# Two attention tiles per visit or one, and blocks of 256 or 512 tokens: a replanned order in a fused scan and two-layer MLP kernel

## The chip, the cores and the metric

The kernel runs on one core of a Trainium2 chip. The metric is the device time of one execution in microseconds; lower is better. The engines are named as in the profile: PE is the matrix engine (PEld its weight loads), DVE, ACT and POOL are the vector, scalar and GpSimd engines, SP is the engine whose queue issues most transfers.

## What is computed

Three stages follow each other on 3072 tokens (batch 4 by sequence 768) of 256 features. The scan works on 8 heads of 32 features with a state of 16 and chunks of 32 tokens; its output feeds the first layer, and that of the first the second, both 256 to 2048 to 256.

```python
# scan, per chunk of 32 tokens
la = log_a[:, :, sl]; cum = np.cumsum(la, axis=-1)
L = np.exp(cum[:, :, :, None] - cum[:, :, None, :]) * causal
M = np.einsum('bhin,bhjn->bhij', Cc, Bc) * L
y[:, :, sl] = M @ xc + np.einsum('bhin,bhnd->bhid', Cc, state) * np.exp(cum)
state = exp(sum(la)) * state + sum_j(B_j x_j * exp(cum[-1] - cum_j))
# layer 1
h = x @ w_in;  g = h * (1.0 / (1.0 + np.exp(-h)));  y = g @ w_out
# layer 2
h = x @ w_in2
P = a[0] + a[1]*h + a[2]*h**2 + a[3]*h**3
Q = 1.0 + abs(b[0])*abs(h) + abs(b[1])*h**2
out = (P / (Q + 1e-6)) @ w_out2
```

The weights come as 64-bit floats. Products are made from a high and a low part of each operand, three matmuls for one.

## The kernel before

**Tiles.** The tokens are cut into 24 tiles of 128, six per batch element. A tile's scan needs POOL and DVE passes (bw; ce, which multiplies by the decay factors; cx; cw), the small matmuls cb and u on PE, and on DVE the masked products M (L671, with the mask Gm of L589), the masked inputs um (L692) and the states S (L707, L709). A *visit* on PE then makes the tile's output from M and S (`att<-M,tok` and `att<-tok,S` in the profile). ACT writes its high part, y1h (L814), DVE its low part, y1l (L817). From visit 5 on, a visit also does cb and u of the tiles of the next visit. VISITS lists which tiles a visit takes: single tiles up to number 7, then pairs.

**Weights.** Each layer has 16 slices of 128 hidden units, 512 KB each. ACT (L490), DVE (L496, L498) and ACT and DVE or POOL (L514, L518) turn a slice into its high and low part; layer 2's slices are written to DRAM (w2s) in that form and loaded again later.

**Layer 1.** BLOCKS groups the tiles: two blocks of 256 tokens and five of 512. For each block and each slice there is an in-projection of six matmuls (`h<-y1h,w`, `h<-y1l,w`), silu on ACT (L900), the split into gh and gl (L856, L862), and an out-projection of six (`acc<-gh,w`, `acc<-gl,w`). Below, such six matmuls are a *group*. Layer 2 has the same shape over six blocks of 512, with ACT, POOL and DVE passes for P, Q and their quotient (DVE lines L968 to L986, twice or more per slice).

**Decay factors.** Per tile, 134 factors per partition, Ee, are needed. For tiles 0 to 2 they are made directly; for the others two products are written to DRAM (dre), and 21 loads of 67 KB, into a ring of four buffers, fetch them (L580).

**The order.** Everything is put into a Plan: an operation with its possible engines, an assumed length, a key, the buffers that it makes and uses. The planner lists the operations by assumed times, and this list is what each engine executes. K holds the numbers from which the keys come. A ring gives out its buffers in turn, and a turn also waits for the first user of the turn before. All transfers at the start are issued by SP, in the order of their keys; the helper `mm` (L290) issues every matmul.

Of the kernel before, what the change touches and what calls it, by code (L numbers as in the profile page):

```python
# [11 lines left out]
AF = mybir.ActivationFunctionType  # L12
# [13 lines left out]
BLOCKS = [2, 2, 4, 4, 4, 4, 4]  # L26
E_DIRECT = 3
NB2 = 512
# [3 lines left out]
    t0=-2912.149,  # L32
    step0=7.448,
    lag1=-799.401,
    fo1=18.905,
    fo2=5644.62,
    fol=22.648,
    tab=-142.05,
    lead=1708.414,
    kt=430.738,  # L40
    kq=-1089.363,
    kl=958.617,
    kg=5975.296,
# [15 lines left out]
    w1=-2845.877,
    w1step=-459.066,  # L60
    w1load=-38.315,
    tokload=151.165,
    ahead=-52.038,
    eps=0.021,
    step2=852.892,
    dT=[244.778, -4327.46, -1277.81, 3.30798e+06, -1852.19, 6.575, 6049.41, 42.655, 11.659, 525.288, -927.012, -29.398, 1118.15, -7033.22, -147.429, -1383.28, 639.647, -92.11, -499.629, -298.276, 63.339, -194.545, 195.77, -178.741],
    dD=[-3949.64, 1922.71, 516.55, -1.95112e+06, -295.737, 604.675, -1987.05, -321.034, -222.002, 1481.65, -774.684, 9639.86, -277.217, -203.799, 192.388, 31257.8, -1529.13, 49.425, -312.61, 173.525, 91.326, 298.355, 2.378, 3.702],
    dW=[1541.58, -222.487, -81.764, 7155.04, -53.883, 106.916, -69.667, -107.809, -443.948, 604.658, -226.317, -95.072, 42.853, 104.916, 101.819, 28.904],
# [17 lines left out]
IN_PSUM = 2  # L86
ALONE = 5
PAIRED = 8
# [30 lines left out]
class Plan:  # L119


    LAT = {"PE": 0.2, "ACT": 0.08, "DVE": 0.08, "POOL": 0.08, "SP": 2.0}
# [11 lines left out]
    def run(self):  # L134
# [3 lines left out]
        for op in self.ops:  # L138
            deps = set(op.deps)
            for b in op.new:  # L140
                i = b.ring.turns.index(b)
                if i:
                    deps.update(b.ring.turns[i - 1].users[:1])
                if i >= b.ring.n:
                    deps.update(b.ring.turns[i - b.ring.n].users)
            deps.discard(op)
            op.waits = deps
            left[op] = len(deps)
            for d in deps:
                waiting.setdefault(d, []).append(op)  # L150
# [73 lines left out]
def ssd_moe_moe_kernel(ctx: ExitStack, tc: tile.TileContext, tok, la_in, consts, w1, w2, ab, outT):  # L224
# [67 lines left out]
    def dma(key, nbytes, fn, deps=(), new=(), use=()):  # L292
        return add({"SP": (max(0.06, nbytes / 345e3), fn)}, key, deps, new, use)
# [26 lines left out]
    ring("Ee", 4, P + R6, pad=26)  # L320
# [34 lines left out]
    ld_la = dma(0.0, 98e3, lambda: (load_table(SET_LN_EXP), nc.sync.dma_start(la, la_in)))  # L355
# [7 lines left out]
    ld_c2 = dma(0.9, 66e3, lambda: nc.sync.dma_start(con[:, C_MASK:C_CUM], consts[:, C_MASK:C_CUM]))  # L363
    ld_ab = dma(0.95, 3e3, lambda: nc.sync.dma_start(abt, ab))
# [49 lines left out]
    o_ee, o_dre, dre = {}, [], fixed("dre", [P, 2, P + R6], space="DR")  # L414
    Ees = {}

    def factors(la_cols, key, after, use=()):
        Ee, pe = new("Ee"), new("h")

        def f_em():  # L420
            pe.t = pe.make()
            mm(pe.t[:, 0 : P + R6], la_cols(), difs, True, True)

        def f_ee():
            Ee.t = Ee.make()
            ACT.activation(Ee.t, pe.t[:, 0 : P + R6], AF.Exp)

        a = add({"PE": (c_mm32(P + R6), f_em)}, key, [o_ln, ld_c1] + after, new=[pe], use=list(use), cols=4 * (P + R6))
        return Ee, add({"ACT": (c_act(P + R6, True), f_ee)}, key, [a], new=[Ee], use=[pe])

    for n in range(E_DIRECT):
# [123 lines left out]
    def attention(n, T, d, k_load):  # L555
# [4 lines left out]
        def f_load():  # L560
            t.t = t.make()
            nc.sync.dma_start(t.t[:, 0:TOK], tok[n])
# [7 lines left out]

        if n < E_DIRECT:
            Ee = Ees[n]
        else:
            Ee = new("Ee")
            i = 0 if n < P // H else 1
            r = (n - i * (NTB - P // H)) * H

            def f_er():
                Ee.t = Ee.make()
                nc.sync.dma_start(Ee.t, dre[r : r + H, i, :].unsqueeze(1).broadcast_to([H, N, P + R6]))  # L580

            o_ee[n] = dma(k_load, 68e3, f_er, [o_dre[i]], new=[Ee])
        e0 = lambda: Ee.t[:, P : P + R6]
# [3 lines left out]
        def f_gm(eng):  # L587
# [10 lines left out]
            T, [o_eG[n], ld_c2], new=[Gm],  # L598
# [9 lines left out]
        def f_ce(eng):  # L608
            eng.tensor_tensor(cw(), cw(), Ee.t[:, 0:P], op=ALU.mult)  # L609
# [52 lines left out]
    def masked(n, cb, o_cb):  # L662
        t, T, d, ld, o_bw, o_cx, o_cw, o_gm, Gm, x, bw, cw, bt, cx, e0, Ee = at[n]
# [22 lines left out]
    def state(n, ub, o_u):  # L686
        t, T, d, ld, o_bw, o_cx, o_cw, o_gm, Gm, x, bw, cw, bt, cx, e0, Ee = at[n]
# [9 lines left out]
        a = add({"DVE": (c_dve(NCH * SW), f_um)}, T + 4.4 * d, [o_u, ld_c2], new=[um], use=[ub], rd=[2, 3])  # L697
        before = states.get(n - 1) if c else None
        here = [before]
        for i in range(NCH if c < TPB - 1 else 1):  # L700
# [11 lines left out]
            b = add({"DVE": (c_dve(SW, ap=1), f_s, True)}, T + 4.5 * d, deps, new=[sn], use=[um] + ([Ee, pv[0]] if pv else []))  # L712
# [58 lines left out]
    def visit(ns):  # L771
# [3 lines left out]
        if n < ALONE:  # L775
# [5 lines left out]
            o_y = add({"PE": (y_len, f_y)}, T + 5 * d, y_deps, new=ybs, use=y_use, wr=range(4), cols=y_cols, big=False)  # L781
# [3 lines left out]
        else:  # L785
# [3 lines left out]
            def f_visit():  # L789
# [7 lines left out]
                {"PE": (y_len + (0.25 + 0.35 * len(after) if after else 0.1), f_visit)}, T + 5 * d,  # L797
# [391 lines left out]
```

## Time and profile before

| | us |
|---|---|
| median of 3 runs (610.09 to 611.59) | 610.37 |
| profiled execution, its own time | 609.46 |
| span of its profile | 607.7 |
| mean granted clock of TensorE | 0.98 |

The profiled execution's time is 1.8 us longer than the span, which runs from its first instruction to its last. Busy times overlap across engines; a PE that is busy may still be working at a lower granted clock, so a stage is read by its busy time, its clock and its waits together.

### The profile page before, as it was taken

What the parts mean: (1) busy time and instruction counts of PE and PEld (TensorE: products, weight loads), DVE (VectorE), ACT (ScalarE), POOL (GpSimd) and SP (SyncE); (2) the same over time, 40 slices, a digit from 0 to 9 for tenths busy, and PEclk for the clock granted to TensorE, in tenths of its full rate; (3) what the DMA queues carried; (4) which work ended last, traced back from release to release, by engine and by line L of the source; (5) the groups of instructions that cost most, each with busy time, mean ns of one, the idle gap of its engine ahead of it and who ended that gap; (6) DMA issues with size and microseconds to landing.
All of it is one profiled execution on the core that took longest, in us unless ns stands there. A gap on an engine that the chain in (4) does not pass through costs nothing.

```text
span 607.7 us, 12571 instructions
## 1 busy us (share of the span) xinstructions
PE 582.2 (96%) x4778; PEld 479.4 (79%) x4781; DVE 435.2 (72%) x800; ACT 437.3 (72%) x858; POOL 280.8 (46%) x313
## 2 busy tenths in 40 slices
PE   7698888988999999999999999999999999999997
PEld 4377788867888888888888888888888888888886
DVE  5988875867852232232222799999999999999995
ACT  4677665755554444444444898998999999999994
POOL 2444323232320010010010589989877787877873
PEclk7889999989999999999999999999999999999999
DMA  6855556374610000000015710000000000000000
GB/s 210 277 182 173 199 212 235 134 265 158 218 73 0 1 0 1 0 2 0 1 69 159 281 46 2 0 36 1 25 12 1 36 1 0 36 0 2 35 1 35
DMA packets 18325, 47.38 MB, mean 78 GB/s; under 512 B 2009, under 2 KB 5465, under 8 KB 18265
## 3 DMA queue, kind: packets, MB, share of 16 engines
q1 hardware_dynamic: 18264, 46.58, 22.4%
q8 instruction: 37, 0.61, 0.4%
q14 instruction: 24, 0.19, 0.1%
HBM read 34.90 MB, written 11.67 MB: 77 GB/s over the span
## 4 chain that ended last, share of the span: by engine, by line
PE 88%; DVE 2%; issue 2%; ACT 2%; DMA 1%; SPq 0%; DVEq 0%; ACTq 0%
PE acc L290 43%; PE h L290 35%; PE b L290 7%; PE att L290 3%; DMA wraw<-in_w_dram 1%; DVE wv L498 1%; ACT wv L490 1%; DVE w L518 0%; ACT y1h L814 0%; ACT w L514 0%; ACT h L900 0%; DVE gl L862 0%; DVE y1l L817 0%; DVE M L671 0%; DVE tok L609 0%
## 5 line engine op out<-in xcount | busy, mean ns | idle before, releaser
L290 PE MATMUL h<-y1h,w 128*128 128x512 f32 (+1 forms) x700 | 229.3, 374 | 6.8 <-DVE gl L862 2.8
L290 PE MATMUL acc<-gh,w 128*128 128x512 f32 (+1 forms) x832 | 211.8, 377 | 0.1
L290 PEld LDWEIGHTS acc<-gh,w 128*128 128x128 f32 x832 | 151.1, 191 | 28.6 <-ACT gh L856 0.3
L290 PEld LDWEIGHTS h<-y1h,w 128*128 128x128 f32 x700 | 130.5, 190 | 32.9 <-DVE gl L862 4.1
L862 POOL TENSOR_TENSOR gl<-g,gh 128x512 fp32r<-128x512 f32 x95 | 122.9, 1294 | 25.1 <-ACT gh L856 22.9
L862 DVE TENSOR_TENSOR gl<-T,gh 128x512 fp32r<-128x512 f32 x71 | 50.0, 704 | 114.8 <-ACT gh L856 112.1
L290 PE MATMUL h<-y1l,w 128*128 128x512 f32 (+1 forms) x350 | 130.1, 372 | 0.8 <-DVE y1l L817 0.5
L290 PE MATMUL acc<-gl,w 128*128 128x512 f32 (+1 forms) x416 | 122.4, 375 | 0.0
L900 ACT ACTIVATE T<-h 128x512 f32<-128x512 f32 x80 | 47.8, 597 | 73.1 <-PE h L290 66.8
L290 PEld LDWEIGHTS acc<-gl,w 128*128 128x128 f32 x416 | 76.8, 190 | 14.0
L965 POOL TENSOR_SCALAR tok<-T,abt 128x512 f32<-128x512 f32 x96 | 74.1, 772 | 22.0 <-ACT T L957 20.9
L858 POOL TENSOR_SCALAR gh<-T 128x512 fp32r<-128x512 f32 x10 | 6.8, 676 | 166.8 <-PE acc L290 163.9
L290 PEld LDWEIGHTS h<-y1l,w 128*128 128x128 f32 x350 | 66.6, 190 | 11.8 <-DVE y1l L817 0.7
L968 DVE SCALAR_TENSOR_TENSOR b<-T,absb,b 128x512 f32<-128x512 f32 x96 | 72.3, 754 | 1.9 <-ACT b L961 0.5
L986 DVE SCALAR_TENSOR_TENSOR g<-tok,abt,b 128x512 f32<-128x512 f32 x96 | 71.1, 742 | 0.3
L977 ACT ACTIVATE b<-b,lnb 128x512 f32<-128x512 f32 x96 | 65.8, 685 | 2.3 <-DVE b L968 1.6
L856 ACT ACTIVATE gh<-T 128x512 fp32r<-128x512 f32 x70 | 44.2, 631 | 25.2 <-PE acc L290 25.1
L980 ACT ACTIVATE b<-b 128x512 f32<-128x512 f32 x96 | 59.7, 622 | 0.5
L856 ACT ACTIVATE gh<-g 128x512 fp32r<-128x512 f32 x71 | 47.5, 670 | 1.6 <-DVE g L986 1.5
L974 DVE SCALAR_TENSOR_TENSOR tok<-T,abt,h 128x512 f32<-128x512 f32 x63 | 46.7, 742 | 0.0
L290 PE MATMUL b<-y1h,w 128*128 128x512 f32 x132 | 46.1, 390 | 0.0
L971 DVE TENSOR_TENSOR h<-tok,h 128x512 f32<-128x512 f32 x63 | 43.4, 689 | 0.0
(72 smaller groups left out, 660.3 us busy)
## 6 DMA issues: line engine op xcount, KB each, us to landing
wraw<-in_w_dram SPq DMA_DIRECT2D x32, 512.0 KB
w2s<-wraw SPq DMA_DIRECT2D x16, 512.0 KB
w<-w2s SPq DMA_DIRECT2D x16, 512.0 KB
tok<-in_tok_dram SPq DMA_DIRECT2D x24, 320.0 KB
out_dram<-wraw SPq DMA_DIRECT2D x12, 256.0 KB
Ee<-dre SPq DMA_DIRECT2D x21, 67.0 KB
cum<-in_consts_dram SPq DMA_DIRECT2D x1, 192.0 KB
dre<-Ee SPq DMA_DIRECT2D x2, 67.0 KB
```

What stands on the lines that cost most here:

```text
L290: PE.matmul(out, lhsT, rhs, start=start, stop=stop)
L856: ACT.activation(gh.t[:, 0:W], g.t[:, 0:W], AF.Copy)
L858: eng.tensor_scalar(gh.t[:, 0:W], g.t[:, 0:W], 1.0, 0.0, op0=ALU.mult, op1=ALU.add)
L862: eng.tensor_tensor(gl.t[:, 0:W], g.t[:, 0:W], gh.t[:, 0:W], op=ALU.subtract)
L900: ACT.activation(T.t[:, 0:W], h.t[:, 0:W], AF.Silu)
L965: POOL.tensor_scalar(t1.t[:, 0:W], s.t[:, 0:W], abt[:, 3:4], abt[:, 1:2], op0=ALU.mult, op1=ALU.add)
L968: DVE.scalar_tensor_tensor(c.t[:, 0:W], s.t[:, 0:W], absb[:, 1:2], c.t[:, 0:W], op0=ALU.mult, op1=ALU.add)
L971: DVE.tensor_tensor(h.t[:, 0:W], t1.t[:, 0:W], h.t[:, 0:W], op=ALU.mult)
L974: DVE.scalar_tensor_tensor(t1.t[:, 0:W], s.t[:, 0:W], abt[:, 2:3], h.t[:, 0:W], op0=ALU.mult, op1=ALU.add)
L977: ACT.activation(c.t[:, 0:W], c.t[:, 0:W], AF.Ln, bias=lnb)
L980: ACT.activation(c.t[:, 0:W], c.t[:, 0:W], AF.Exp, scale=-1.0)
L986: DVE.scalar_tensor_tensor(g.t[:, 0:W], t1.t[:, 0:W], abt[:, 0:1], c.t[:, 0:W], op0=ALU.add, op1=ALU.mult)
```

## The change

It sets six blocks of 512 tokens in layer 1 (SH, the number of 256-token blocks, becomes 0, and IN_PSUM with it) and one tile per visit throughout. All decay factors lie in one fixed tile, Ea; tiles 0 to 2 are made there directly, and four loads bring the rest, for tiles 3 to 5, 6 to 9, 10 to 15 and 16 to 23. The layout of dre is by head and tile. The transfer of cum and of tile 0 is issued on ACT's queue, ahead of its table load; con comes in one transfer. The rule of the rings waits for the start, not the end, of the first user of the turn before. Assumed lengths of transfers and visits are a little higher, and the numbers of K are others (two of some hundred are shown). The lines of the changed kernel are 4 to 9 higher, so `mm` is L294 there.

```diff
-BLOCKS = [2, 2, 4, 4, 4, 4, 4]
+BLOCKS = [4, 4, 4, 4, 4, 4]
+SH = 2 if BLOCKS[:2] == [2, 2] else 0
+E_LOADS = [(3, 6), (6, 10), (10, 16), (16, 24)]
...
-    t0=-2912.149,
+    t0=-79.407,
...
-IN_PSUM = 2
+IN_PSUM = SH
-PAIRED = 8
...
-    LAT = {"PE": 0.2, "ACT": 0.08, "DVE": 0.08, "POOL": 0.08, "SP": 2.0}
+    LAT = {"PE": 0.2, "ACT": 0.08, "DVE": 0.08, "POOL": 0.08, "SP": 2.6}
...
-            deps = set(op.deps)
+            deps, first = set(op.deps), set()
...
-                    deps.update(b.ring.turns[i - 1].users[:1])
+                    first.update(b.ring.turns[i - 1].users[:1])
...
-                        q: max(d.end + (self.LAT[d.eng] if d.eng != q or q == "SP" else self.SELF[q]) for d in o.waits)
+                        q: max(
+                            [d.end + (self.LAT[d.eng] if d.eng != q or q == "SP" else self.SELF[q]) for d in o.waits]
+                            + [d.start for d in o.first]
+                        )
...
-        return add({"SP": (max(0.06, nbytes / 345e3), fn)}, key, deps, new, use)
+        return add({"SP": (max(0.33, nbytes / 345e3), fn)}, key, deps, new, use)
...
-    ring("Ee", 4, P + R6, pad=26)
...
-    ld_c1 = dma(0.1, 70e3, lambda: nc.sync.dma_start(con[:, 0:C_MASK], consts[:, 0:C_MASK]))
+    ld_con = add({"SP": (0.4, lambda: nc.sync.dma_start(con, consts[:, 0:C_CUM]))}, 0.1)
...
-        nc.sync.dma_start(cum.t[:, 0 : C_CEND - C_CUM], consts[:, C_CUM:C_CEND])
+        nc.scalar.dma_start(cum.t[:, 0 : C_CEND - C_CUM], consts[:, C_CUM:C_CEND])
...
-    o_ee, o_dre, dre = {}, [], fixed("dre", [P, 2, P + R6], space="DR")
-    Ees = {}
+    o_ee, o_dre, dre = {}, [], fixed("dre", [H, NTB, P + R6], space="DR")
+    Ea = fixed("Ea", [P, NTB * (P + R6) + 48])
+    Ev = Ea[:, 0 : NTB * (P + R6)].rearrange("p (n e) -> p n e", n=NTB)
...
-            nc.sync.dma_start(t.t[:, 0:TOK], tok[n])
+            (nc.sync if n else nc.scalar).dma_start(t.t[:, 0:TOK], tok[n])
+            if n == 0:
+                load_table(SET_LN_EXP)
...
-                nc.sync.dma_start(Ee.t, dre[r : r + H, i, :].unsqueeze(1).broadcast_to([H, N, P + R6]))
+                    nc.sync.dma_start(Ev[:, n0:n1, :], dre[:, n0:n1, :].unsqueeze(1).broadcast_to([H, N, n1 - n0, P + R6]))
...
-            eng.tensor_tensor(cw(), cw(), Ee.t[:, 0:P], op=ALU.mult)
+            eng.tensor_tensor(cw(), cw(), Ev[:, n, 0:P], op=ALU.mult)
...
-    VISITS = [[n] for n in range(PAIRED)] + [[n, n + 1] for n in range(PAIRED, NTB, 2)]
+    VISITS = [[n] for n in range(NTB)]
...
-                {"PE": (y_len + (0.25 + 0.35 * len(after) if after else 0.1), f_visit)}, T + 5 * d,
+                {"PE": (y_len + (0.3 + 0.36 * len(after) if after else 0.15), f_visit)}, T + 5 * d,
...
-        shared = b < 2
+        shared = b < SH
```

How the order moves shows at three places. The first is PE at the first layer-1 group, h_466 before and h_516 now (w_22 and w_19 are weight tiles; the rows on T are filler matmuls). Before:

```order
L290 MATMUL att_80<-M_322,tok_179 32x64 x8
L290 MATMUL att_81<-M_322,tok_179 32x64 x8
L290 MATMUL att_80<-tok_179,S_349 32x64 x4
L290 MATMUL att_81<-tok_179,S_349 32x64 x4
L290 MATMUL att_80<-tok_179,S_386 32x64 x4
L290 MATMUL att_81<-tok_179,S_386 32x64 x4
L290 LDWEIGHTS T_91
L290 MATMUL acc_73<-T_91 128x512
...
L290 MATMUL h_466<-y1h,w_22_263 128x256
L290 MATMUL h_466<-y1l,w_22_263 128x256
L290 MATMUL h_466<-y1h,w_22_263 128x256 x2
L290 MATMUL h_466<-y1l,w_22_263 128x256
```

Now:

```order
L294 MATMUL att_80<-M_399,tok_113 32x64 x8
L294 MATMUL att_81<-M_399,tok_113 32x64 x8
L294 MATMUL att_80<-tok_113,S_264 32x64 x4
L294 MATMUL att_81<-tok_113,S_264 32x64 x4
L294 MATMUL att_80<-tok_113,S_348 32x64 x4
L294 MATMUL att_81<-tok_113,S_348 32x64 x4
L294 MATMUL att_81<-tok_350 32x64 x8
L294 LDWEIGHTS T_225
L294 MATMUL acc_73<-T_225 128x512
...
L294 MATMUL h_516<-y1h,w_19_363 128x512
L294 MATMUL h_516<-y1l,w_19_363 128x512
L294 MATMUL h_516<-y1h,w_19_363 128x512 x2
```

Before, the group is of 256 tokens and comes behind the visits of tiles 0 to 2 (tok_179 is tile 2); now it is of 512 and comes behind those of tiles 0 to 3 (tok_113 is tile 3) and the u of tile 4 (tok_350).

The second is a visit on PE in the later part of layer 1. Before, the last visit but one: tok_2508 and tok_2570 are its tiles (20 and 21), tok_2737 and tok_2782 the next two, whose cb and u it does first.

```order
L290 MATMUL att_81<-tok_2737 32x64 x8
L290 MATMUL att_81<-tok_2782 32x64 x8
L290 MATMUL att_80<-M_2751,tok_2508 32x64 x8
L290 MATMUL att_81<-M_2751,tok_2508 32x64 x8
L290 MATMUL att_80<-M_2756,tok_2570 32x64 x8
L290 MATMUL att_81<-M_2756,tok_2570 32x64 x8
L290 MATMUL att_80<-tok_2508,S_2566 32x64 x4
L290 MATMUL att_81<-tok_2508,S_2566 32x64 x4
L290 MATMUL att_80<-tok_2508,S_2784 32x64 x4
L290 MATMUL att_81<-tok_2508,S_2784 32x64 x4
L290 MATMUL att_80<-tok_2570,S_2787 32x64 x4
```

Now, a visit of one tile, tok_718, with cb and u of the next, tok_1106, and the group behind it:

```order
L294 MATMUL att_80<-tok_1106 64x128 x2
L294 MATMUL att_81<-tok_1106 64x128 x2
L294 MATMUL att_81<-tok_1106 32x64 x8
L294 MATMUL att_80<-M_1290,tok_718 32x64 x8
L294 MATMUL att_81<-M_1290,tok_718 32x64 x8
L294 MATMUL att_80<-tok_718,S_1217 32x64 x4
L294 MATMUL att_81<-tok_718,S_1217 32x64 x4
L294 MATMUL att_80<-tok_718,S_1304 32x64 x4
L294 MATMUL att_81<-tok_718,S_1304 32x64 x4
L294 MATMUL acc_72<-gh_1272,w_70_984 128x512
L294 MATMUL acc_73<-gh_1272,w_70_984 128x512
```

A visit's rows are half as many, and a group follows after each.

The third is SP's queue from the start (tok_98 is tile 0 before; tok_97, tok_100 and tok_113 are tiles 1 to 3 now). Before:

```order
L355 DMA la<-in_la_dram 128x192
L356 DMA con<-in_consts_dram 128x136
L360 DMA cum_95<-in_consts_dram 128x384
L562 DMA tok_98<-in_tok_dram 128x640
L477 DMA wraw_105<-in_w_dram 128x512
L363 DMA con<-in_consts_dram 128x128
L364 DMA abt<-in_ab_dram 128x6
L562 DMA tok_126<-in_tok_dram 128x640
L477 DMA wraw_146<-in_w_dram 128x512
L562 DMA tok_179<-in_tok_dram 128x640
L447 DMA dre<-Ee_194 128x134
L477 DMA wraw_203<-in_w_dram 128x512
```

Now:

```order
L358 DMA la<-in_la_dram 128x192
L359 DMA con<-in_consts_dram 128x264
L572 DMA tok_97<-in_tok_dram 128x640
L572 DMA tok_100<-in_tok_dram 128x640
L572 DMA tok_113<-in_tok_dram 128x640
L487 DMA wraw_122<-in_w_dram 128x512
L366 DMA abt<-in_ab_dram 128x6
L487 DMA wraw_146<-in_w_dram 128x512
L455 DMA dre<-T_158 16x8x134
L487 DMA wraw_186<-in_w_dram 128x512
L455 DMA dre<-T_223 8x8x134
L587 DMA Ea<-dre 128x1x402
```

Tiles 1 to 3 now stand ahead of the first weight, cum and tile 0 are gone from this queue, and the four loads of decay factors stand together behind the third weight.

## Rows read from the trace of the kernel before

**Rows 1.** The busy line of the page.

```profile
PE 582.2 (96%) x4778; PEld 479.4 (79%) x4781; DVE 435.2 (72%) x800; ACT 437.3 (72%) x858; POOL 280.8 (46%) x313
```

**Rows 2.** Windows by stage: span, busy us (instructions) of PE, PEld, DVE, ACT, POOL, clock, DMA, GB/s.

```profile
0.00:25.90 25.90, 18.27 (x344) 10.19 (x347) 17.66 (x44) 13.83 (x35) 9.45 (x18) 0.80 0.73 233
25.90:182.20 156.30, 142.08 (x2575) 120.30 (x2576) 117.87 (x304) 98.92 (x245) 51.30 (x71) 0.96 0.55 189
...
182.20:339.60 157.40, 157.40 (x696) 130.32 (x695) 41.17 (x60) 73.07 (x119) 6.36 (x8) 1.00 0.09 29
339.60:599.40 259.80, 259.80 (x1148) 215.03 (x1147) 257.10 (x392) 250.23 (x460) 213.04 (x218) 1.00 0.07 26
```

**Rows 3.** Chain of waits, in time: start us, length us, engine.

```profile
73.98 0.72 PE acc L290 x6
...
162.87 2.51 PE att L290 x157
165.38 1.59 PE acc L290 x6
...
182.39 1.36 PE h L290 x6
...
604.11 0.69 DVE wraw L1025
```

**Rows 4.** Timeline of PE at a single visit: start us, us, engine, line.

```profile
43.35 0.75 PE L290 MATMUL att<-tok 32*64 32x128 f32 x32
...
44.79 0.75 PE L290 MATMUL acc<-gh,w 128*128 128x256 f32 x4
...
45.61 0.28 PE L290 MATMUL h<-y1h,w 128*128 128x256 f32 x1
```

**Rows 5.** What PE waits for, 25.9 to 182.2: us in total, times, longest.

```profile
PE att L290 <- issue: 7.1, 4, 2.2
PE h L290 <- DVE gl L862: 2.8, 3, 1.1
PE h L290 <- ACT y1h L814: 1.8, 1, 1.8
```

**Rows 6.** Timeline of PE at a pair visit's hole; transfers from 138 to 139, by queue.

```profile
138.37 0.74 PE L290 MATMUL att<-tok,S 32*32 32x64 f32 x51
140.64 0.34 PE L290 MATMUL att<-tok,S 32*32 32x64 f32 x13 [1.53 <-issue]
...
q8 instruction: 1, 0.02, 6.6%
```

**Rows 7.** Timelines of PE and ACT: the first layer-1 group, the first weight's pass.

```profile
25.90 0.39 PE L290 MATMUL h<-y1h,w 128*128 128x256 f32 x1 [1.81 <-ACT y1h L814]
...
7.91 0.66 ACT L490 ACTIVATE wv<-wraw 128x512 f32<-128x512 f32 x1 [1.77 <-DMA wraw<-in_w_dram]
```

**Rows 8.** DMA issues of the page.

```profile
tok<-in_tok_dram SPq DMA_DIRECT2D x24, 320.0 KB
```

**Rows 9.** DVE by line, 0 to 182, forms apart: busy, mean ns; DVE's timeline, two merges.

```profile
L498 DVE SCALAR_TENSOR_TENSOR wv<-wraw,wv 128x512 uint32<-128x512 uint32 x32 | 22.0, 689 | 0.2
L671 DVE TENSOR_TENSOR M<-att,Gm 128x256 f32<-128x256 f32 x48 | 19.0, 417 | 0.7 <-PE att L290 0.3
L496 DVE TENSOR_SCALAR wv<-wv 128x512 uint32<-128x512 uint32 x32 | 15.5, 483 | 5.7 <-ACT wv L490 5.6
L709 DVE SCALAR_TENSOR_TENSOR S<-S,Ee,um 128x64 f32<-128x64 f32 x40 | 14.1, 352 | 0.1
...
L817 DVE TENSOR_TENSOR y1l<-att,y1h 128x128 fp32r<-128x128 f32 x48 | 11.8, 285 | 6.8 <-ACT y1h L814 6.1
L589 DVE TENSOR_TENSOR Gm<-eG,con 128x512 f32<-128x512 f32 x14 | 10.0, 713 | 1.4 <-DMA con<-in_consts_dram 1.4
...
12.94 1.28 DVE L498 SCALAR_TENSOR_TENSOR wv<-wraw,wv 128x512 uint32<-128x512 uint32 x2
```

**Rows 10.** Timeline of DVE: the last pass of the last layer-1 weight.

```profile
69.03 0.69 DVE L518 TENSOR_TENSOR w<-wv,w 128x512 fp32r<-128x512 f32 x1
```

More of the change, by code (lines that the diff above doesn't have):

```diff
@@ L59 @@
[L59 to L67, printed above, removed]
@@ L68 @@
-    dW=[1541.58, -222.487, -81.764, 7155.04, -53.883, 106.916, -69.667, -107.809, -443.948, 604.658, -226.317, -95.072, 42.853, 104.916, 101.819, 28.904],
+    t0=-79.407,
+    step0=1854.239,
+    lag1=-388.588,
+    fo1=14.021,
+    fo2=91910.096,
+    fol=17.22,
+    tab=86.658,
+    lead=6771.146,
+    kt=-91.784,
+    kq=-231.718,
+    kl=9369.024,
+    kg=777.377,
+    ks=-1218.959,
+    warm=23,
+    warm0=-12511.44,
+    warmstep=52.604,
+    late=-103.321,
+    tab0=35.047,
+    bulk=462.298,
@@ new lines @@
+    d0=-17739.661,
+    gap0=-702.503,
+    d2=-33911.521,
+    d3=-2507.589,
+    early2=-269.33,
+    early=6750.168,
+    w2a=-242.762,
+    w2b=205.502,
+    w1=-58140.669,
+    w1step=1941.777,
+    w1load=4358.83,
+    tokload=-189.053,
+    ahead=-62.753,
+    eps=0.058,
+    step2=5080.625,
+    dT=[-34.651, -466.345, -1375.83, 566.477, -11.633, 141.036, 574.911, 9213.26, -1613.35, -292.251, -241.094, -49.132, 3220.28, 307.353, -405.771, -3949.3, -20.416, 41.978, 41.387, -341.084, -338.025, -33.415, 39.986, 94.735],
@@ L146, in run @@
             deps.discard(op)
-            op.waits = deps
-            left[op] = len(deps)
-            for d in deps:
+            op.waits, op.first = deps, first - deps - {op}
+            left[op] = len(deps) + len(op.first)
+            for d in list(deps) + list(op.first):
                 waiting.setdefault(d, []).append(op)
@@ L413, in ssd_moe_moe_kernel, with factors @@
     decays(0, 4, 1.0, [])
-    o_ee, o_dre, dre = {}, [], fixed("dre", [P, 2, P + R6], space="DR")
-    Ees = {}
-    def factors(la_cols, key, after, use=()):
-        Ee, pe = new("Ee"), new("h")
+    o_ee, o_dre, dre = {}, [], fixed("dre", [H, NTB, P + R6], space="DR")
+    Ea = fixed("Ea", [P, NTB * (P + R6) + 48])
+    Ev = Ea[:, 0 : NTB * (P + R6)].rearrange("p (n e) -> p n e", n=NTB)
+    def factors(la_cols, key, after, n, use=()):
+        Ee, pe = new("T") if n is None else None, new("h")
+        out = lambda: Ev[:, n, :] if Ee is None else Ee.t[:, 0 : P + R6]
         def f_em():
@@ L424, in f_ee @@
         def f_ee():
[L425 to L429, printed above, removed]
+            if Ee:
+                Ee.t = Ee.make()
+            ACT.activation(out(), pe.t[:, 0 : P + R6], AF.Exp)
+        a = add({"PE": (c_mm32(P + R6), f_em)}, key, [o_ln, ld_con] + after, new=[pe], use=list(use), cols=4 * (P + R6))
+        return Ee, add({"ACT": (c_act(P + R6, True), f_ee)}, key, [a], new=[Ee] if Ee else [], use=[pe])
     for n in range(E_DIRECT):
@@ L569, in attention, with f_er @@
         cx = lambda: t.t[:, TOK : TOK + DM]
[L571 to L579, printed above, removed]
-                nc.sync.dma_start(Ee.t, dre[r : r + H, i, :].unsqueeze(1).broadcast_to([H, N, P + R6]))
-            o_ee[n] = dma(k_load, 68e3, f_er, [o_dre[i]], new=[Ee])
-        e0 = lambda: Ee.t[:, P : P + R6]
+        for n0, n1 in E_LOADS:
+            if n == n0:
+                def f_er(n0=n0, n1=n1):
+                    nc.sync.dma_start(Ev[:, n0:n1, :], dre[:, n0:n1, :].unsqueeze(1).broadcast_to([H, N, n1 - n0, P + R6]))
+                first, end = n0 * H // P, (n1 - 1) * H // P
+                o = dma(k_load, 67e3 * (n1 - n0), f_er, o_dre[first : end + 1])
+                o_ee.update(dict.fromkeys(range(n0, n1), o))
+        e0 = lambda: Ev[:, n, P : P + R6]
         Gm = new("Gm")
@@ L695, in f_um @@
             )
-        a = add({"DVE": (c_dve(NCH * SW), f_um)}, T + 4.4 * d, [o_u, ld_c2], new=[um], use=[ub], rd=[2, 3])
+        a = add({"DVE": (c_dve(NCH * SW), f_um)}, T + 4.4 * d, [o_u, ld_con], new=[um], use=[ub], rd=[2, 3])
         before = states.get(n - 1) if c else None
@@ L711, in state @@
             deps = [a] if pv is None else [a, pv[1], o_ee[n]]
-            b = add({"DVE": (c_dve(SW, ap=1), f_s, True)}, T + 4.5 * d, deps, new=[sn], use=[um] + ([Ee, pv[0]] if pv else []))
+            b = add({"DVE": (c_dve(SW, ap=1), f_s, True)}, T + 4.5 * d, deps, new=[sn], use=[um] + ([pv[0]] if pv else []))
             here.append((sn, b))
@@ L723, in cb_alone @@
         cb, f_cb = cb_part(n)
-        o_cb = add({"PE": (0.35, f_cb)}, T + 2 * d, o_cx, new=[cb], use=[t], wr=range(4), cols=4 * P, big=False)
+        o_cb = add({"PE": (0.37, f_cb)}, T + 2 * d, o_cx, new=[cb], use=[t], wr=range(4), cols=4 * P, big=False)
         masked(n, cb, o_cb)
```

71 lines of the change are left out of this document (25 added, 46 removed).

## The prediction

> **What bounds the kernel now.** I read the busy line of the page first, then the windows by stage, then the chain of waits, then single rows of the engines. The busy line [rows 1] has PE at 96% of the span and every other engine at 72% or less, so the time is PE's work plus the moments when PE has none. The windows [rows 2] say where those moments are. From 182.2 to 599.4 PE is busy for every microsecond, at a granted clock of 1.00. Before that it is not: in the first 25.9 us no layer-1 group runs, and from 25.9 to 182.2 PE is busy for 142.08 of 156.30 us, at a mean clock of 0.96. So a change can gain in the first 182 us, by less PE work, by fewer empty moments, or by an earlier start; behind that only the amount of PE work counts, and the last piece after PE's end.
>
> The chain [rows 3] gives the prices. A group of six matmuls is 0.72 us at 256 tokens and 1.36 us at 512. A pair visit (attention of two tiles) is 2.51 us, and the group behind it takes 1.59 instead of 1.36, so it costs 2.51 + 0.23 = 2.74. The last copy begins at 604.11 in a span of 607.7, so 3.6 us lie behind PE's end. Of a single visit the PE timeline [rows 4] shows 1.44 us from its first matmul (43.35) to the next group's (44.79), and that 256-token group lasts 0.82 instead of 0.72. That makes 1.54; with the pair's 0.23 it would be 1.67. I take 1.65, nearer to the row with 512-token groups around it, as the changed kernel has.
>
> The waits of PE between 25.9 and 182.2 [rows 5] have one large item: 7.1 us in four pieces put down to "issue", PE waiting for nothing that the profile shows. One is in [rows 6]: in a pair visit, 51 of 64 state products are done, then 1.53 us pass, then the last 13. A 0.02 MB packet of the instruction queue was the only transfer in the microsecond from 138 to 139, just before. All four are in the eight pair visits (windows around the other three have such a packet too), and none is in the five single visits that follow the first group. A pair visit of some 150 small matmuls, with as many weight loads, runs through PE's instructions faster than any other stretch.
>
> **The sum for the kernel before, by these prices.** First group at 25.9 [rows 7]; 64 groups of 256 tokens (16 slices, two blocks, in and out) x 0.72 = 46.1; 352 of 512 x 1.36 = 478.7; visits 3 to 23, which are 5 x 1.65 + 8 x 2.74 = 30.2; end 3.6. Together 584.5 of the span of 607.7. The other 23.2 are the four holes (7.1), the named waits (2.8, 1.8, 1.2 and smaller ones, about 8 [rows 5]), the lower clock ((1 - 0.96) x 156 = 6 [rows 2]), and 2 that I can't place.
>
> **The change, part by part.**
>
> *Blocks.* Two of 256 tokens become one of 512. The 64 x 0.72 = 46.1 us become 32 x 1.36 = 43.5: a gain of 2.6. Beside PE, DVE's and ACT's small passes over 256 tokens go too, which costs nothing while PE bounds.
>
> *Visits.* Visits 0 to 3 now come ahead of the first group, where before it was 0 to 2. So 20 visits lie between groups: 20 x 1.65 = 33.0 instead of 30.2, a loss of 2.8 (bounds 20 x 1.54 and 20 x 1.67: 30.8 to 33.4). In PE's own work, then, the two parts cancel.
>
> *Holes.* A single visit issues about half as many small matmuls in one run, and large groups follow it. By the 5 single visits without a hole beside 4 holes in 8 pair visits, I take all 7.1 as gone. The bounds: none left, or, if each visit had the pair's risk, 20 x 4/8 x 7.1/4 = 17.7 us of them, which the single visits speak against.
>
> Here a rule speaks against this gain. The Trainium skill, page "Runtime: NRT & Kernel Launch", section "Instruction fetch mechanics", says that the sequencer fetches the next block of instructions while it executes the current one, and that crossing a block's end is "mostly hidden". By that the holes would have another cause and could stay, and the sum would be some 7 higher. The trace speaks against it with 1.53 us right behind an instruction packet [rows 6].
>
> *Decay factors.* 21 loads of 67 KB and their ring of four buffers become four loads into one fixed tile, with the same bytes. SP issues 17 transfers less, and SP's queue is in none of the waits of [rows 5], so I count 0. The passes that read the tile have the same shapes as before: 0.
>
> *First transfers and order.* The first group's start is the term that I know least. It needs all four tiles through attention, and one weight. The transfers now go la, con, tiles 1 to 3, first weight on SP, with cum and tile 0 on ACT's queue. Before, the first weight lay behind one tile and was in use at 7.91 [rows 7]. Now it lies behind four tiles of 320 KB [rows 8], 1 MB more, about 3 us at the start's 233 GB/s [rows 2], less where two queues move more. DVE therefore begins its weight passes at about 10. From there to the last y1l that the first group needs, DVE's list holds 3 merges, 4 bit passes, 3 mask products Gm, 2 passes lo, 8 M, 8 S, 4 um, 8 y1l and 2 small ones. By the means of [rows 9] that is 17.9 us (um as y1l, lo as merge). Rows that follow each other overlap: two merges take 1.28 [rows 9], not 1.38, and with 0.09 less for each of the 42 passes it is 14.1. So the start is at 24.1 to 28; I take 26.5, above the middle because PE and ACT pass the two pairs of tiles back and forth in between. Against 25.9 that is a loss of 0.6.
>
> *Waits in the stage of the weights.* The last layer-1 weight was ready at 69.7 [rows 10], so DVE delivered one per 3.6 us from about 15. DVE now has no 256-token pieces there, and its passes for the first block (M, S, um, y1l, Gm of tiles 4 to 7, and twelve weights) come to 30 to 37 us against PE's 36. That is close to balance. The order lets PE do in-projections of new slices and their out-projections from the start of one 512-token block, so each weight brings 2.72 us of PE work at once, where a slice of 256 brought 1.44. I take the rest of waits and lost clock as 8, about half of the 8 + 6 + 2 before. Bounds: 3 (only the small items of [rows 5]) and 16 (all of it stays).
>
> *Layer 2 and the tail.* The groups are the same in number, 192 x 1.36. In the 259.80 us in which DVE does its 96 slices of layer 2 it is busy for 257.10 [rows 2], 2.68 a slice, and PE needs 2.72. The kinds and shapes of the passes are as before. I count 0, and keep a rival for it.
>
> **Sum.** 26.5 + 384 x 1.36 (522.2) + 33.0 + 8 + 3.6 = 593.3 of span. The profiled execution took 609.46 beside a span of 607.7, so 1.8 lie around it: 595.1. The median of the runs (610.37) stands 0.9 above the profiled one; I forecast **595.0**, between 594 and 596. The forecast's own bounds: start 24, waits 3, visits 30.8 give 585.4; start 28 and waits 16 give 605.
>
> **Rivals.**
>
> 1. *Weights pace the first block.* PE is done with each slice in 2.72 and waits for the next, at 3.6 apart. 12 slices x 0.9 = 10 us, of which attention (4 visits x 1.65) fills 4 to 5, so 6 more: 601. For it: that was the pace before [rows 10]; against: DVE has fewer and larger passes beside the weights now. Chance 0.13.
> 2. *Holes stay*: what stopped PE was not the packet but something that single visits meet too: 595 + 7 = 602. For it: PE's small products are as many as before. Against: none in five single visits. The Trainium skill's section above is on this rival's side. Chance 0.10.
> 3. *Late start.* Tile 4's load waits for a buffer of visit 0, and weight 3 stands behind it in SP's queue; with the first weights late too, the first group starts at 30 and PE waits 4 more for slice 3: 602. Chance 0.07.
> 4. *Slower: layer 2 turns to DVE.* The replanned order puts a wait into the 96 slices. DVE has 0.04 us of room per slice; each 0.01 beyond it costs 0.96 us. A wait of 0.08 still leaves 599; from 0.20 a slice (DVE at 2.88) the gain of 15.4 is gone, and at 0.23 the time is 613. For it: the order's rules changed for every stage. Against: the same passes, and DVE idle for only 2.7 of these 259.80 us before. Chance 0.04.
> 5. *Nothing gained*: PE's end is set by something else that I don't see, or the weights' stage gives back all: 610. Chance 0.03.
>
> **How the numbers follow.** The forecast has 0.63. A measurement of this kernel can tell about 0.3%, 1.8 us, so everything under 608.5 counts as faster: the forecast and rivals 1 to 3, 0.93; same 0.03; slower 0.04. The range holds 8 in 10 from 586.5 (below it about 0.04) to 603.5, which takes in the three faster rivals' middles and leaves out their upper halves, 0.08, and the last two, 0.07.
>
> **What would show it.** Right: a first layer-1 group at 24 to 28; no group of 256; single visits of 1.5 to 1.7; "issue" under 2 us behind the start; waits for weights of 2 to 6 us in the first block; PE busy without a gap from about 165; layer 2 again 2.72 a slice. Wrong, each by its own sign: many waits of PE for DVE's w before 70 (rival 1); holes of 1.5 us or more inside single visits (rival 2); a first group at 30 (rival 3); PE waiting for gl or gh in layer 2 (rival 4).

## The result and the profile after

The changed kernel takes 595.48 us (median of 4 runs, 593.44 to 596.07) against 610.80 for the kernel before in the same comparison; the ratio is 0.9743, 95% interval 0.9715 to 0.9771. The forecast was 595.0, in a range of 586.5 to 603.5. The profiled execution took 594.96 with a span of 593.2, so 1.8 us lie around the span, as before.

The busy line of its page, the counterpart of [rows 1]:

```profile
PE 578.4 (98%) x4586; PEld 465.1 (78%) x4589; DVE 437.4 (74%) x782; ACT 433.3 (73%) x823; POOL 284.0 (48%) x317
```

PE's busy time fell by only 3.8 us (582.2 to 578.4), while the span fell by 14.5 (607.7 to 593.2): the other 10.7 us of the gain are time in which PE had no work. Windows of the changed kernel, cut at the first layer-1 group and behind the last visit (columns as in [rows 2]):

```profile
0.00:30.33 30.33, 20.34 (x427) 12.53 (x430) 16.84 (x46) 14.07 (x39) 8.88 (x21) 0.95 0.78 246
30.33:76.00 45.67, 45.55 (x472) 35.55 (x472) 41.84 (x89) 34.48 (x71) 15.34 (x18) 0.96 0.54 180
76.00:161.80 85.80, 84.87 (x1813) 63.84 (x1805) 70.78 (x184) 53.83 (x128) 37.61 (x49) 1.00 0.53 180
161.80:589.60 427.80, 427.60 (x1883) 353.16 (x1883) 307.42 (x467) 330.86 (x589) 222.13 (x229) 1.00 0.11 37
```

What PE waits for from 30.3 to the end of the span is two short items, where [rows 5] had 7.1 us of issue alone:

```profile
PE acc L294 <- POOL wraw L528: 0.9, 1, 0.9
PE h L294 <- ACT y1h L823: 0.2, 1, 0.2
```

So from 30.3 on the holes are gone, and the waits for gl and for the first block's weights with them; the 0.9 us for a weight's pass are at 161.33, behind the last visit. (A piece of issue of 0.83 us lies ahead of the first group, at 24.47.) The start, though, is late. Timeline of PE around the first layer-1 group, then at a single visit between groups of 512:

```profile
28.31 0.47 PE L294 MATMUL att<-tok 64*32 64x64 f32 x16 [3.01 <-POOL tok L612]
...
30.33 0.79 PE L294 MATMUL h<-y1h,w 128*128 128x512 f32 x1 [0.15 <-ACT y1h L823]
...
78.53 0.39 PE L294 MATMUL h<-y1h,w 128*128 128x512 f32 x1
...
79.98 0.75 PE L294 MATMUL att<-tok 32*64 32x128 f32 x32
...
81.43 1.19 PE L294 MATMUL acc<-gh,w 128*128 128x512 f32 x4
...
82.92 0.39 PE L294 MATMUL h<-y1h,w 128*128 128x512 f32 x1
```

The visit itself is 1.45 us (79.98 to 81.43), the group behind it 1.49 and the one in front 1.45, instead of 1.36: 1.67 in all. The first group begins at 30.33, not at 25.90 [rows 7], and PE stood 3.01 us before it, waiting for tile 4. Timelines of SP, POOL, ACT and DVE at that place:

```profile
12.64 3.18 SPq L587 DMA_DIRECT2D Ea<-dre  x4
17.50 0.33 SPq L572 DMA_DIRECT2D tok<-in_tok_dram  x1
...
27.86 0.40 POOL L612 TENSOR_TENSOR tok<-tok,eL 128x128 f32<-128x128 f32 x1 [6.62 <-DMA tok<-in_tok_dram]
...
28.71 0.69 ACT L625 ACTIVATE tok<-tok,con 128x128 f32<-128x128 f32 x2 [8.15 <-POOL tok L618]
...
29.99 0.60 DVE L506 TENSOR_SCALAR wv<-wv 128x512 uint32<-128x512 uint32 x1 [6.16 <-ACT wv L500]
```

Tile 4's load is issued at 17.50, behind the four loads of decay factors, and POOL gets it at 27.86: ten us, where the page's median from issue to landing of such a load is 3.8. Every engine then stands behind tile 4 in its own order: POOL for 6.62 us, ACT for 8.15, DVE for 6.16, and ACT's y1h and DVE's y1l of tiles 2 and 3, which the first group needs, are listed behind that.

### The profile page after: what moved, and what is told of

Same layout as the page of the kernel before. It is cut to its first block, busy times and chain, and to the rows that moved or that the text cites. A ratio compares the mean times of both kernels' runs of the same rounds, so it can differ in the third digit from the quotient of the medians.

```text
span 593.2 us, 12129 instructions
## 1 busy us (share of the span) xinstructions
PE 578.4 (98%) x4586; PEld 465.1 (78%) x4589; DVE 437.4 (74%) x782; ACT 433.3 (73%) x823; POOL 284.0 (48%) x317
## 4 chain that ended last, share of the span: by engine, by line
PE 72%; DVE 0%; issue 0%
PE acc L294 37%; PE h L294 28%; PE b L294 8%; DVE wraw L1034 0%
## 5 line engine op out<-in xcount | busy, mean ns | idle before, releaser
L294 PE MATMUL h<-y1h,w 128*128 128x512 f32 x636 | 222.0, 394 | 0.2 <-ACT y1h L823 0.2
L294 PE MATMUL acc<-gh,w 128*128 128x512 f32 x768 | 206.7, 391 | 1.0 <-POOL wraw L528 0.9
L294 PEld LDWEIGHTS acc<-gh,w 128*128 128x128 f32 x768 | 143.5, 188 | 31.8 <-issue 1.3
L294 PEld LDWEIGHTS h<-y1h,w 128*128 128x128 f32 x636 | 119.9, 189 | 27.1 <-ACT y1h L823 1.1
L294 PE MATMUL h<-y1l,w 128*128 128x512 f32 x318 | 124.5, 392 | 0.1
L294 PE MATMUL acc<-gl,w 128*128 128x512 f32 x384 | 118.5, 389 | 0.0
L909 ACT ACTIVATE T<-h 128x512 f32<-128x512 f32 x96 | 57.0, 595 | 72.3 <-PE h L294 72.1
L867 POOL TENSOR_SCALAR gh<-T 128x512 fp32r<-128x512 f32 x17 | 13.9, 818 | 157.9 <-PE acc L294 128.0
L294 PEld LDWEIGHTS acc<-gl,w 128*128 128x128 f32 x384 | 72.1, 188 | 15.1
L294 PEld LDWEIGHTS h<-y1l,w 128*128 128x128 f32 x318 | 60.0, 189 | 12.6 <-DVE y1l L826 0.6
L865 ACT ACTIVATE gh<-T 128x512 fp32r<-128x512 f32 x79 | 49.8, 631 | 21.4 <-PE acc L294 21.1
L294 PE MATMUL b<-y1h,w 128*128 128x512 f32 x132 | 46.1, 390 | 0.0
```

The costliest lines, as they stand in the source:

```text
L294: PE.matmul(out, lhsT, rhs, start=start, stop=stop)
L865: ACT.activation(gh.t[:, 0:W], g.t[:, 0:W], AF.Copy)
L867: eng.tensor_scalar(gh.t[:, 0:W], g.t[:, 0:W], 1.0, 0.0, op0=ALU.mult, op1=ALU.add)
L909: ACT.activation(T.t[:, 0:W], h.t[:, 0:W], AF.Silu)
```

## The experiments

**Do the holes come from long runs of small products?** Three runs. The first (split_pairs) leaves the order of the kernel before and takes half of each pair visit one group forward:

```diff
-            def f_visit():
-                for _, f in cbs + us:
-                    f()
-                f_mx()
-                f_cs()
+            def f_visit():
+                f_mx()
+                f_cs()
+            def f_next():
+                for _, f in cbs + us:
+                    f()
...
```

The part left out calls `f_next` ahead of the last PE operation before a pair visit, where its inputs allow it.

> The kernel before, with the same order, but in each pair visit the cb and u products of the next pair are issued one group earlier, so that six large matmuls cut the run of small ones in two. Theory A (PE runs out of fetched instructions in a long run of small products): the four holes of 1.5 to 2.2 us put down to issue, 7.1 us together, shrink to at most one; each cut adds some 0.2 us to a visit, 8 x 0.2 = 1.6, so 610.4 - 7.1 + 1.6 = 605 us (603 to 607). Rival B (the holes have another cause in pair visits): the holes stay, 610 to 613 us.

Measured: 608.09 us against 611.16, ratio 0.9955 (0.9931 to 0.9978). PE's timeline shows four pieces of issue inside the visits, beside one of 0.63 in a group at 62.18:

```profile
88.89 0.34 PE L291 MATMUL att<-tok,S 32*32 32x64 f32 x16 [0.56 <-issue]
...
104.83 0.41 PE L291 MATMUL att<-tok,S 32*32 32x64 f32 x20 [1.94 <-issue]
...
123.54 0.45 PE L291 MATMUL att<-tok,S 32*32 32x64 f32 x29 [1.13 <-issue]
...
138.45 0.34 PE L291 MATMUL att<-tok,S 32*32 32x64 f32 x14 [0.49 <-issue]
```

They sit in the same four visits, but hold 4.1 us instead of 7.1; the time fell by 3.1. Neither branch is right as written: six large matmuls in the middle shorten a hole by 0.3 to 1.0 us each and don't remove it.

The second (visits_long) makes the single visits of the changed kernel as long as a pair's:

```diff
-                for _, f in cbs + us:
+                for _, f in (cbs + us) * 3:
```

> The changed kernel, with the cb and u products of the next tile issued three times over in every visit from 5 on (the same values are written again), so a single visit's run of small products is about as long as a pair's. Repeated work: 18 visits x 2 x 0.75 us = 27, so without holes 595.5 + 27 = 622 us (617 to 626). Theory A: holes of 1.5 us or more under issue come back inside the visits, in about half of them, 18 x 0.5 x 1.8 = 16 us, so 638 us (630 to 645). Rival B: no holes, 617 to 626 us.

Measured: 628.15 us (ratio 1.0313, 1.0256 to 1.0370), and six pieces of issue, 6.0 us together, in the visits, two of which are:

```profile
154.54 0.35 PE L294 MATMUL att<-M,tok 64*32 64x64 f32 x17 [2.40 <-issue]
...
168.71 0.33 PE L294 MATMUL att<-tok,S 32*32 32x64 f32 x10 [1.59 <-issue]
```

Holes come back with single tiles, as theory A said, but in a third of the visits and mostly shorter than I took: 622 + 6 = 628. So it is the number of products in a run that matters, not the pairing of tiles.

The third (pairs_again) goes back to pairs from tile 8 on in the changed kernel:

```diff
-    VISITS = [[n] for n in range(NTB)]
+    VISITS = [[n] for n in range(8)] + [[n, n + 1] for n in range(8, NTB, 2)]
```

> The changed kernel with VISITS as before (single up to tile 7, then pairs), its order planned again; the start is the same. Prices: 16 single visits at 1.67 become 8 pairs at 2.74, 4.8 us less. Theory A: two to six holes come back, about 7 us, so 595.5 - 4.8 + 7 = 598 us (594 to 601). Rival B (the holes went because of the new order, not of the single visits): no holes and 590 to 592 us, faster than the changed kernel.

Measured: 598.84 us (594.47 to 599.53; ratio 0.9790, 0.9744 to 0.9837). Two holes are back in pair visits, and a piece of 0.33:

```profile
109.47 0.69 PE L294 MATMUL att<-tok,S 32*32 32x64 f32 x46 [1.44 <-issue]
...
122.84 0.41 PE L294 MATMUL att<-tok,S 32*32 32x64 f32 x19 [1.95 <-issue]
```

That is theory A's sign, and rules out rival B, that the new order took the holes away. By time theory A's 598 fits the median; but the profile is that of the fastest execution (594.47), so the 4.4 us from there to the median are not explained by these holes. The intervals of this run and of the changed kernel overlap: single visits are worth 3.4 us by the medians, which is not clear of the noise.

*What ends a hole* can be read from the traces. Count PE's matmuls and weight loads together, from the start, as PE instructions. Windows of the kernel before that end inside its first two holes give the numbers of both kinds:

```profile
0.00:87.90 87.90, 71.71 (x1492) 56.40 (x1496) 69.30 (x182) 57.48 (x151) 32.13 (x50) 0.90 0.62 204
0.00:104.30 104.30, 85.92 (x1748) 69.96 (x1751) 79.18 (x211) 66.75 (x176) 38.45 (x58) 0.90 0.63 210
```

That is 2988 and 3499 instructions, and 4011 and 4521 at the other two holes: 510 to 512 apart. An instruction packet comes for every 255 to 258 of them (37 for 9559 before, 36 for 9175 in the changed kernel, 45 for 11479 in visits_long), so the holes lie two packets apart. And each ends nearly the same time behind the landing of a packet, by the packets' own records in the traces:

| run | PE instructions ahead of the hole | packet landed, us | hole ended, us | between |
|---|---|---|---|---|
| before | 2988 | 86.70 | 88.02 | 1.32 |
| before | 3499 | 103.06 | 104.47 | 1.41 |
| before | 4011 | 122.18 | 123.59 | 1.41 |
| before | 4521 | 139.33 | 140.64 | 1.31 |
| visits_long | 6309 | 153.08 | 154.54 | 1.46 |
| visits_long | 7075 | 167.28 | 168.71 | 1.43 |
| pairs_again | 3754 | 121.60 | 122.84 | 1.24 |

In all twelve traces 20 pieces of issue of 0.45 us or more lie behind 20 us; each ends 1.2 to 1.6 us behind a packet, and the count ahead of each is a multiple of 256 plus 162 to 185. Where the packet landed 1.6 us or more before PE came to such a place, there is no piece of issue. So PE stood for its next instructions, as theory A says.

The numbers also say why pair visits have holes. PE ran through the last 256 instructions ahead of each of the four holes in about 1.5 us (137.61 to 139.11 at the fourth). The packet began 0.7 to 1.5 us after the start of these 256, took 0.9 to 1.0, and the hole ended 1.3 to 1.4 later. In 512-token groups 256 instructions take 29 us (427.60 us for 1883 matmuls, as many weight loads). A pair visit has 314 instructions [rows 3], a lengthened single visit 320, an ordinary one 192: the first two can hold 256 in one run, the third can't. A hole had one more price: behind two of the four the granted clock was at its lower level for 3.4 us (89.6 to 93.0 and 123.7 to 127.2).

```profile
89.70:93.00 3.30, 3.30 (x18) 3.30 (x17) 2.38 (x9) 1.25 (x5) 3.10 (x3) 0.50 0.99 386
123.80:127.10 3.30, 3.30 (x35) 2.55 (x17) 2.50 (x11) 1.63 (x5) 0.70 (x1) 0.50 0.99 224
```

**What do the parts do alone?** The kernel before with single visits only (before_single), planned again:

> The kernel before with VISITS changed to single tiles throughout, its order planned again with its own numbers. Prices: 8 pair visits at 2.74 become 16 at 1.67, 4.8 us more; Theory A: the four holes (7.1 us) go, so 610.4 + 4.8 - 7.1 = 608 us (605 to 611). Rival B: holes stay, 615 us.

Measured: 617.61 us, ratio 1.0124 (1.0084 to 1.0165), slower than before. From 25.9 to the end PE has no issue hole left, but these waits, beside smaller ones:

```profile
PE h L290 <- DVE gl L862: 6.8, 4, 2.6
PE att L290 <- DVE y1l L817: 2.5, 1, 2.5
PE h L290 <- ACT y1h L814: 1.8, 1, 1.8
```

The 7.1 us of holes went, and waits for gl (6.8 where [rows 5] has 2.8) and for y1l came. Single visits need an order made for them; with the numbers of the kernel before they lose.

The changed kernel with two blocks of 256 tokens (after_256), planned again:

```diff
-BLOCKS = [4, 4, 4, 4, 4, 4]
+BLOCKS = [2, 2, 4, 4, 4, 4, 4]
```

> The changed kernel with BLOCKS as before (two of 256 tokens, then five of 512), its order planned again with the changed kernel's numbers. The smaller groups cost 64 x 0.72 - 32 x 1.36 = 2.6 us more. If the blocks matter by PE's work alone: 598 us (596 to 600). If the first stage's waits and lost clock of the kernel before came with the small blocks (a weight brings 0.72 us of work at a time while DVE delivers one per 3.6): 601 to 608 us, with PE's waits for weights and for gl between 30 and 80 at 5 us or more.

Measured: 611.80 us, ratio 1.0027 (1.0004 to 1.0050): all of the gain is gone, and more than either branch had. What PE waits for between 25 and 182, and the window from 25 to 80:

```profile
PE acc L294 <- DVE gl L871: 4.1, 6, 1.4
PE acc L294 <- ACT gh L865: 2.9, 2, 2.3
...
PE h L294 <- DVE w L528: 1.4, 2, 1.0
...
25.00:80.00 55.00, 46.16 (x946) 36.54 (x946) 44.72 (x113) 37.10 (x100) 25.82 (x36) 0.88 0.60 196
```

PE is idle for 8.8 of 55 us there, and the mean clock is 0.88, worth at most (1 - 0.88) x 55 = 6.6. The same window of the changed kernel:

```profile
25.00:80.00 55.00, 51.39 (x617) 39.25 (x607) 45.34 (x99) 38.07 (x81) 19.56 (x26) 0.94 0.56 189
```

It has 3.6 us idle, 3.0 of them the wait for tile 4, and a clock of 0.94; from 30.33 to 76 it has 0.1 and 0.96. And this although the smaller block starts ten us earlier (first group at 20.20). The larger first block, with an order made for it, is thus worth far more than the 2.6 us of PE work that I gave it. How much of the 16 us is the block and how much is an order whose numbers were made for another, these runs don't separate; the same holds for the run before this one.

**Is the late start a loss?** Three of the four loads of decay factors are moved back in SP's queue, each behind the transfer of the rank in LATE_E, and every engine's order stays as it is. The ranks shown are those of the third of three runs:

```diff
+LATE_E = (17, 35, 39)
...
+    order = plan.run()
...
+    spq = [op for op in order if op.eng == "SP" and op not in loads]
+    for op, behind in zip(loads, LATE_E):
+        order.remove(op)
+        order.insert(order.index(spq[behind]) + 1, op)
...
```

The first (late_decay, ranks 17, 21 and 25) placed them badly:

> The changed kernel, with three of the four loads of decay factors (tiles 6 to 23) moved back in SP's queue, behind later weights, and nothing else moved. In the changed kernel the load of tile 4 is issued at 17.50 and landed at 27.6, and PE, ACT, DVE and POOL all stand behind tile 4 before the first layer-1 group at 30.33. Theory C (these loads hold tile 4 back, and the late start is a loss of its own): tile 4 lands by 23, the first group is at 26 to 27, PE's waits behind it stay under 2.5 us, 595.5 - 3.5 = 592 us (590.5 to 593.2). Rival D (the weights pace the first block, and the late start only takes the place of waits): the first group is earlier, but PE's waits behind it grow by as much, 594.5 to 596.5 us. Rival E (tile 4 is late for another reason): first group still at 29 to 31, 595 to 596.5 us.

Measured: 598.26 us (ratio 0.9800, 0.9759 to 0.9840). The load for tiles 10 to 15 had gone ahead of the one for tiles 6 to 9, so ACT stood 3.04 us behind tile 6. PE also had the longest hole of all runs, ahead of a packet that landed at 29.65:

```profile
31.26 0.45 PE L295 MATMUL att<-tok 32*64 32x128 f32 x8 [2.77 <-issue]
```

The first group came at 25.30 and the end 3.6 us later than in the changed kernel's profile (596.8 to 593.2): with two losses of its own it says nothing on the question. The second (late_decay2) had the three in order of tile, at ranks 17, 32 and 33:

> The changed kernel with the loads of decay factors moved in SP's queue alone: those for tiles 6 to 9 behind the fifth weight, for 10 to 15 behind the thirteenth, for 16 to 23 behind the fourteenth; every engine's order is unchanged. (In late_decay the load for tiles 10 to 15 went first, so that tile 6's factors came late and ACT stood 3.0 us behind tile 6; this run mends that.) Theory C (the late start is a loss of its own): first group at 25 to 26, PE's waits behind it under 2.5 us, 591 us (590 to 593). Rival D (weights pace the first block, so that an earlier start only makes PE wait later): first group at 25 to 26, PE's waits behind it 4 us or more, within 1.5 us of the control.

Measured beside the changed kernel on the same chip: 597.83 us (ratio 0.9805, 0.9769 to 0.9841) to 595.52 (0.9762, 0.9728 to 0.9796), intervals that overlap; both spans are 593.9. The first group came at 24.96, and at the 12th slice ACT's silu was 3.7 us ahead (59.7 to 63.4), at the 16th 1.8 behind (82.0 to 80.2). By numbers this was rival D; the profile showed another cause, in ACT's timeline where two weights came late:

```profile
63.48 0.66 ACT L501 ACTIVATE wv<-wraw 128x512 f32<-128x512 f32 x1 [3.17 <-DMA wraw<-in_w_dram]
68.38 0.68 ACT L501 ACTIVATE wv<-wraw 128x512 f32<-128x512 f32 x1 [3.72 <-DMA wraw<-in_w_dram]
```

These weights stood behind the two moved loads (issued at 53.50 and 55.83). The third (late_decay3) put those loads behind all layer-1 weights:

> As late_decay2, but the decay factors for tiles 10 to 15 stand behind the last layer-1 weight in SP's queue, and those for tiles 16 to 23 behind the load of tile 13, so that no weight waits behind them (in late_decay2 the lead of 3.7 us at the 12th slice was lost between 60 and 82, where ACT waited 3.17 and 3.72 us for weights behind these loads). Theory C (the late start is a loss of its own, and late_decay2 lost its lead to the moved loads): first group at 25, the lead of 3.7 us or more is kept past 82, span 590 (589 to 591.5), 4 us under the control. Rival D (the passes over the weights pace the first block, so the lead shrinks anyway): the lead at the 16th slice is under 1.5 us and the span within 1.5 us of the control's 593.9.

> The changed kernel again, unaltered, on the same chip as late_decay3. All theories: 594 to 597 us, span 593 to 594.5.

Measured: 591.89 us (588.70 to 592.54; ratio 0.9677, 0.9645 to 0.9709), the changed kernel beside it 594.96 (0.9745, 0.9711 to 0.9779); the profiles' spans are 588.8 and 593.7. PE's and POOL's timelines of late_decay3:

```profile
25.24 0.59 PE L295 MATMUL h<-y1h,w 128*128 128x512 f32 x1
...
21.56 0.40 POOL L613 TENSOR_TENSOR tok<-tok,eL 128x128 f32<-128x128 f32 x1
...
30.00:40.00 10.00, 9.36 (x191) 7.14 (x190) 9.85 (x21) 7.71 (x18) 3.77 (x5) 1.00 0.55 195
```

The last row is its window from 30 to 40. Beside the changed kernel on the same chip, POOL has tile 4 5.2 us earlier (26.80 there), the first group comes 4.0 us earlier (29.28), and the lead at the 16th slice is 5.4 (74.9 to 80.3). Some of it is the clock: in two windows of the changed kernel's first profile

```profile
20.00:30.00 10.00, 5.41 (x155) 2.56 (x154) 3.45 (x12) 1.85 (x8) 2.51 (x5) 0.85 0.98 302
30.00:40.00 10.00, 9.73 (x228) 6.52 (x228) 9.78 (x23) 8.10 (x20) 5.08 (x7) 0.81 0.38 128
```

it is 0.85 and then 0.81, a mix of its two levels, where PE was busy for only 5.41 of the first 10 us; in late_decay3, where PE was not kept waiting for tile 4, it is 1.00. Theory C holds: the late start was a loss of its own, and moving three transfers gives 3.1 us by the medians (4.9 by the profiles). It is the fastest of the versions tried.

**A control** ran beside late_decay2, the changed kernel unaltered:

> The changed kernel itself, unaltered, on the same chip as the three others of this set. All theories: 594 to 597 us, first layer-1 group at about 30, no hole of 1.4 us in a visit.

Measured: 595.52 us, first group at 29.31, span 593.9, and no hole in a visit.

## Why the prediction was right, step by step

The span's sum was 593.3 and the span is 593.2, but two terms missed by about 4 us each and cancelled. The range was earned by the pricing of PE's work and of the holes; the agreement to 0.1 us is luck.

| term | predicted | measured |
|---|---|---|
| first layer-1 group | 26.5 | 30.3 (29.3 in both later profiles of this kernel) |
| 384 groups x 1.36 | 522.2 | 522.2 (427.60 us for 1883 matmuls, six a group, are 1.36 each) |
| 20 single visits | 33.0 | 20 x 1.67 = 33.4, by the price of one |
| waits and lost clock | 8 | 593.2 - 30.3 - 522.2 - 33.4 - 3.7 = 3.6, what the other rows leave |
| behind PE's end | 3.6 | 593.2 - 589.47 = 3.7 |

- *Signs*: of those that I named for being right, the single visits (1.45 to 1.67), issue under 2 us, PE without a gap from 161.8 on and layer 2's 2.72 a slice came. The first group at 24 to 28 and the waits for weights of 2 to 6 us did not; and a first group at 30, the sign of rival 3, came without its 602 us, since the 4 us for slice 3 that it adds were not there.
- *Holes*: right that single visits lose them, and right on the mechanism: longer runs bring holes back, a cut shortens them, and every hole ends 1.2 to 1.6 us behind a packet. The changed kernel has no issue piece of over 1 us on PE. What decides is whether 256 PE instructions pass in one quick run, which the prediction did not have; a single visit can still have a hole where the packet is late, as at 90.38 in late_decay3. The mean of a hole in long single visits was 1.0 us, not the 1.8 that I took from the pairs.
- *The Trainium skill's rule* (page "Runtime: NRT & Kernel Launch", section "Instruction fetch mechanics"), that crossing a block's end is "mostly hidden", holds for most packets here: 36 packets and no hole of a microsecond between layer-1 groups. It fails in runs of small products: 4 holes of 1.5 to 2.2 us among 37 packets before. So the holes have the packets for a cause, against rival 2.
- *Decay factors, "so I count 0"*: this step failed. I checked that SP's queue was in no wait of the kernel before, and not what the four loads, now together, would be ahead of. They cost 3.1 us by the medians and 4.9 by the profiles of late_decay3 and the run beside it. I had tile 4 as rival 3, but by another cause: a buffer of visit 0. That buffer did hold the load until 17.50; the ten us behind that were the transfers in front of it.
- *First group at 24.1 to 28*: the DVE list that I priced was done at 23.8; the last four y1l stood behind tile 4's pieces, which I hadn't counted as part of the list. With tile 4 in time it starts at 25.24, inside the bounds. One step of the working is wrong: 1 MB at 233 GB/s is 4.2 us, not 3; DVE's first weight pass came at 10.55, so the "about 10" held all the same.
- *Blocks, "a gain of 2.6"*: too small. Beside it the term for waits and lost clock was too large: of 16 us or so (8 + 6 + 2), 3.6 remain, not half. after_256 brings back 8.8 us of idle and up to 6.6 of lost clock between 25 and 80, so most of this goes with the block, or with an order made for it, which stays open. Some of the lost clock was not a term of its own: 2 x 3.4 us at half the clock followed holes, 3.4 of the 6.
- *Weights as the pace (rival 1)*: PE waited for no weight's pass in the first block. DVE was busy for 9.78 of 10 us from 30 to 40, so the balance that I saw was real, but it held.
- *Layer 2*: as forecast, PE is busy for 427.60 of 427.80 us from 161.8 on, and rival 4 didn't come.

## What to carry to other kernels

When loads are gathered into a few large ones, look at what now stands behind them on the same queue, and put what is needed late behind what is needed early: one late tile stopped four engines here, since each had a piece of that tile next in its order. A run of small matmuls is safer when it is shorter than what one instruction packet brings, here some 256 matmuls and weight loads together. A first block that gives PE twice the work for each weight can be worth far more than its matmul count says, where weights come at about PE's pace: 16 us went with it here, though an order made for other blocks has a part in that which no run separates. A sum that comes out right is not proof of its terms; check each against the new trace.

## What the runs showed of the hardware

Runs of small matmuls can stop PE for up to 2.8 us (late_decay) with nothing in the profile that it waits for; the hole ends 1.2 to 1.6 us behind the landing of an instruction packet, at places some 256 PE instructions apart. Whether one of these places has a hole is not fixed by the program: late_decay3 has the same order on PE as the changed kernel, and one hole that the other lacks, at instruction 2733, in a single visit.

```profile
90.38 0.34 PE L295 MATMUL att<-M,tok 64*32 64x64 f32 x13 [1.30 <-issue]
```

Its packet began at 87.34, 3.0 us after PE had passed the place before; in the changed kernel the packet for the same instruction began 0.9 us after (89.49 to 90.34), in time. From 85 to 88 late_decay3's data transfers had a DMA share of 0.71. Whether such traffic makes the packet late was not tried.
